# The third block of tokens, not the first, gets eight products; gated weights are converted one place sooner

## The chip, the cores and the metric

The kernel runs on one core of one Trainium2 chip. The metric is device time in microseconds (us), the median of several runs. The profile comes from one profiled execution, which had a time of its own.

## The reference

```python
# retention: q, k, v are (2, 8, 768, 64); a state of 64 x 64 a head, faded each step
state = gamma * state + einsum('bhd,bhe->bhde', k[:, :, t], v[:, :, t])
y[:, :, t] = scale * einsum('bhd,bhde->bhe', q[:, :, t], state)
x = y.transpose(0, 2, 1, 3).reshape(1536, 512)
# first network: w_in 512 x 2048, w_out 2048 x 512
h = x @ w_in
x = (maximum(h, 0) + log1p(exp(-abs(h)))) @ w_out
# second network: w_gate and w_val 512 x 1536, w_out 1536 x 512
rms = sqrt(mean(x * x, axis=-1) + 1e-6)
xn = x / rms * rms_g
g = xn @ w_gate
out = (g / (1 + exp(-g)) * (xn @ w_val)) @ w_out
```

The weights are stored in 64 bits, q, k, v and rms_g in 32.

## The kernel before, in words

The 1536 tokens are three blocks (b = 0, 1, 2) of 512. Every operand of a large product is split in a high and a low part in a rounded 32-bit format, and a product is three terms, high by high, high by low and low by high (TERMS). A weight tile comes as 64-bit words through one of three staging tiles; ScalarE (ACT), VectorE (DVE) and GpSimd (POOL) turn it into high and low parts in one of 11 or 12 slots (`convert`: `shift`, `bits`, `small`, `size`, `total`, `finish`, `high`, `rounded`).

The work is written out by hand as a row of pieces. A piece is one group of products on TensorE (PE), given to `piece()`, which lets due work go out (`run` by a running clock, `flush`), starts a conversion if asked (`conv`), and then writes the readers of the piece's products. Each engine takes its instructions in the order in which this writes them. A piece of 12 products advances that clock by 2.72, one of 6 by 1.36; it is only a due time for `later`.

Stage 1 is the retention. Stage 2 is the first network, in four groups (gr) of four of the 16 slices f of w_in and w_out: for each group and block four `l1` (w_in and softplus) and, one block behind, four `l2` (w_out, m = 0 to 3). The sums of block 0 stay in four PSUM banks through all groups (`keep`, list `kept`); those of blocks 1 and 2 are added up in SBUF (L556). After the last group `norm` takes the squares, their sum (`sums`, L593), the root of the mean (`mean`: a PE product, then 12 short DVE instructions), and spreads it over the partitions (`along`).

Stage 3 is the second network, in six rounds p of two slices. Blocks 1 and 2 share their products: for w_gate and for w_val seven products of half depth (`Seven`, p1 to p7) stand for the eight that two blocks need. They take sums of the weights (`combine`: tiles s, then ws_s) and sums and differences of the blocks (B11, B21, T1 to T4, B22), which `plain` and `mixing` make once, from `scaled` blocks. Block 0 is alone and takes its eight products (`l3`, tiles h_w_gate and h_w_val, four pieces a round); its rows are scaled after the product. `l4` multiplies by the second w_out, `to_g` splits its operand.

For an odd slice of w_gate or w_val `convert` asks for three free slots: its own and two for the sums. If a piece needs a weight that isn't ready, `need` writes all outstanding work of its conversion on the spot, ahead of the piece. `finish` is due 4.0 after the start, `high` 1.0 later, `combine` 0.9 after `finish`, and `parts` 2.7 after `combine`: there ACT takes the high parts of the sums, and DVE the low parts of both weights (L217, `rounded` on DVE). A round asks for conversions in pieces 0 and 2 of its `l3`, pieces 3 and 8 of w_gate's seven products and 2 and 8 of w_val's.

Of the kernel before, what the change touches and what calls it, by code (L numbers as in the profile page):

```python
# [20 lines left out]
G1 = 4  # L21
# [4 lines left out]
def retention_softplus_swiglu(ctx: ExitStack, tc: tile.TileContext, q, k, v, w_in, w_out,  # L26
# [133 lines left out]
    clock, due, raw = [0.0], [], {}  # L160
# [13 lines left out]
    def convert(parts=False):  # L174
# [6 lines left out]
        if len(free) < (3 if gated and f % 2 else 1):  # L181
            return False
# [26 lines left out]
        if gated and f % 2:  # L209
            sums, sa = [], [row(f"s{n}", "s") for n in range(2)]  # L210
            for n in range(2):
                slot["S", nm, f // 2, n] = free.pop(0)
                sums.append(rows(slot["S", nm, f // 2, n], f"ws_s{n}"))
                ws["S", nm, f // 2, n] = sums[n]
# [12 lines left out]
        def combine():  # L227
# [10 lines left out]
            def parts():  # L238
                for n in range(2):
                    high(sums[n], sa[n])  # L240
# [3 lines left out]
                ready.add(key)  # L244

# [5 lines left out]
            later(2.7, parts)  # L251
# [218 lines left out]
    bg = []  # L470
    normed = set()
# [48 lines left out]

    def l2_by(b, f):
        for m in range(KC):
# [3 lines left out]
            for n, (i, j) in enumerate(TERMS):  # L526
                nc.tensor.matmul(acc[b, m], lhsT=w[:, i, m * P:(m + 1) * P], rhs=g_t[b, f][:, j, :],  # L527
                                 start=(n == 0 and f == 0), stop=False)
        g_t.pop((b, f))
        return lambda: None  # L530

    def l2(b, gr, m):
        fs = range(gr * G1, (gr + 1) * G1)
        keep = b == 0
        if keep:
            p = acc[b, m]
        else:
            p = bank("l2")
# [10 lines left out]
        def after():  # L549
            if not keep:  # L550
                if gr == 0:
                    tags[b, m] = spin("s2_", 10)
                    acc[b, m] = row(tags[b, m], "x2")
                    nc.scalar.activation(out=acc[b, m], in_=p, func=AF.Copy)
# [14 lines left out]
    def norm(b, m):  # L569
        if m == 0:  # L570
            root[b], roots[b] = get("root") if b == 2 else (row(("r", "ms")[b], "root"), "ms")
            sqs[b] = [rows(f"at{2 * (b % 2) + n}", "sq", F32) for n in range(2)]
            if b == 0:
                channels(("n", b), b)
        sq, r = sqs[b], root[b]

        def high():
            if b == 0:
# [4 lines left out]
        def low():  # L583
# [3 lines left out]
            if m == KC - 1:  # L587
                normed.add(b)
# [23 lines left out]
        def along():  # L612
# [4 lines left out]
            rooted.add(b)  # L617

# [13 lines left out]
    TB, roots = {}, {}  # L632
    homes = {"B11": ("x4", "x5"), "B21": ("x6", "x7"), "T1": ("x8", "x9"), "B22": ("x10", "x11"),
# [19 lines left out]
    def mixing():  # L653
# [5 lines left out]
        def first():  # L659
            scaled(2, k1)  # L660
            for n in range(2):
                diff(acc[1, n], acc[2, n], acc[1, n])

        def second():
            for n in range(2):
                part_hi("T1", n, acc[1, n])
            scaled(2, k2)

        def third():
            for n in range(2):  # L670
                part_lo("T1", n, acc[1, n])
# [488 lines left out]
```

## Time and profile before

| | us |
|---|---|
| median of 3 runs (653.99 to 654.61) | 654.55 |
| profiled execution | 654.71 |
| its span | 653.0 |
| TensorE busy in the span | 613.4 (94%) |
| VectorE | 450.6 (69%) |
| ScalarE | 359.7 (55%) |
| GpSimd | 284.5 (44%) |

Stage 2 ends and stage 3 begins at about 325 us; the rounds of stage 3 follow each other from about 379 us to the end. The profile's busy time of TensorE counts a product from its start to its modelled end. Durations in the timeline overlap: a row of four instructions of 0.69 us that starts at 325.57, with the next row at 328.22, is 0.66 us from start to start. The granted clock is 1.00 at 2.4 GHz and 0.50 at 1.2 GHz.

### The profile page before, as it was taken

Reading aid. Unit: us, or ns where it says so; the run is one execution under the profiler, and the core shown is the slowest. Engines: PE = TensorE matmul, PEld = TensorE weight load, DVE = VectorE, ACT = ScalarE, POOL = GpSimd, SP = SyncE. Lnnn points to the kernel's source line nnn. Section 1 sums busy time; section 2 is a strip of 40 time slices with the busy share of each in tenths; the row PEclk is TensorE's granted clock in tenths of the full one; section 3 lists DMA queues with packets and bytes.
Section 4 is the critical chain, followed back from the end, with each engine's and each line's share of the span. In section 5 each row is a group of like instructions: output and inputs, shape, how many; then the busy total and the mean of one; then the engine's idle time right before and its main releaser. Section 6 shows DMA issues by size and latency. Waiting matters only on the chain.

```text
span 653.0 us, 8618 instructions
## 1 busy us (share of the span) xinstructions
PE 613.4 (94%) x3232; PEld 503.9 (77%) x3232; DVE 450.6 (69%) x645; ACT 359.7 (55%) x613; POOL 284.5 (44%) x236
## 2 busy tenths in 40 slices
PE   8999999999999999999957787998998998998997
PEld 7888888888888888888846465886886886886886
DVE  5787776777636763575568965489689579679635
ACT  3466677887747774775354644644543453544421
POOL 3444355454403440220053976267367358248210
PEclk9999999999999999999977987999998998999999
DMA  9997133232302230200011022222212121221014
GB/s 207 216 238 184 34 97 114 80 98 96 97 0 65 96 98 1 64 2 0 1 61 36 21 78 65 64 65 64 66 64 63 46 69 50 66 64 65 1 44 150
DMA packets 65562, 48.84 MB, mean 75 GB/s; under 512 B 39792, under 2 KB 60528, under 8 KB 65520
## 3 DMA queue, kind: packets, MB, share of 16 engines
q1 hardware_dynamic: 64320, 47.90, 26.1%
q8 instruction: 25, 0.41, 0.3%
q10 hardware_dynamic: 1200, 0.39, 0.2%
q14 instruction: 17, 0.14, 0.1%
HBM read 45.14 MB, written 3.15 MB: 74 GB/s over the span
## 4 chain that ended last, share of the span: by engine, by line
PE 79%; DVE 13%; POOL 5%; issue 1%; ACT 1%; DMA 1%; SPq 0%; DVEq 0%; POOLq 0%
PE h L478 20%; PE l L542 18%; PE l L858 12%; PE Q L760 9%; PE h_w_val L478 3%; PE R L760 3%; PE y L439 3%; PE W L760 2%; DVE a L254 2%; PE sc L387 2%; DVE g L738 2%; POOL c L204 2%; PE l L527 2%; PE pt L368 1%; DVE w L196 1%
## 5 line engine op out<-in xcount | busy, mean ns | idle before, releaser
L204 POOL TENSOR_TENSOR c<-w,c 128x512 uint32<-128x512 uint32 x68 | 87.8, 1292 | 182.2 <-DVE w L200 121.5
L478 PE MATMUL h<-x,ws_w_in 128*128 128x512 f32 x576 | 138.7, 390 | 0.0
L542 PE MATMUL l<-g,ws_w_out 128*128 128x512 f32 x528 | 126.5, 390 | 0.0
L478 PEld LDWEIGHTS h<-x,ws_w_in 128*128 128x128 f32 x576 | 107.7, 188 | 23.0 <-issue 0.7
L542 PEld LDWEIGHTS l<-g,ws_w_out 128*128 128x128 f32 x528 | 98.9, 188 | 20.5
L858 PE MATMUL l<-ws_w_out,g 128*128 128x512 f32 x432 | 113.1, 403 | 0.0
L858 PEld LDWEIGHTS l<-ws_w_out,g 128*128 128x128 f32 x432 | 84.7, 196 | 18.3
L516 DVE SCALAR_TENSOR_TENSOR t<-h,t 128x512 f32<-128x512 f32 x48 | 33.1, 690 | 72.1 <-ACT t L509 72.1
L217 POOL TENSOR_TENSOR ws_w_out<-a,ws_w_out 128x512 fp32r<-128x512 f32 x28 | 37.3, 1332 | 69.5 <-ACT ws_w_out L220 69.5
L254 DVE SCALAR_TENSOR_TENSOR a<-a,c 128x512 f32<-128x512 f32 x68 | 52.0, 765 | 18.0 <-POOL c L204 18.0
L478 PE MATMUL h_w_val<-x,ws_w_val 128*128 128x512 f32 x144 | 41.4, 436 | 22.6 <-DVE ws_w_val L217 21.7
L478 PEld LDWEIGHTS h_w_val<-x,ws_w_val 128*128 128x128 f32 x144 | 30.0, 213 | 32.2 <-DVE ws_w_val L217 24.2
L124 ACT ACTIVATE g<-t 128x512 fp32r<-128x512 f32 x48 | 30.3, 632 | 38.5 <-DVE t L516 38.5
L504 ACT ACTIVATE t<-h 128x512 f32<-128x512 f32 x48 | 28.7, 598 | 36.1 <-PE h L478 35.8
L125 DVE TENSOR_TENSOR g<-t,g 128x512 fp32r<-128x512 f32 x48 | 33.7, 704 | 12.3 <-ACT g L124 9.4
L760 PE MATMUL Q<-T,ws_s 128*128 128x512 f32 x144 | 37.3, 393 | 4.1 <-ACT p L766 1.6
L888 DVE TENSOR_TENSOR o<-l,o 128x512 f32<-128x512 f32 x39 | 26.7, 686 | 20.1 <-PE l L858 19.9
L781 POOL TENSOR_TENSOR t<-t,e 128x512 f32<-128x512 f32 x18 | 26.3, 1461 | 32.6 <-DVE e L777 32.6
L766 ACT ACTIVATE p<-Q 128x512 f32<-128x512 f32 x36 | 21.4, 596 | 32.9 <-PE Q L760 32.9
L478 PE MATMUL h_w_gate<-x,ws_w_gate 128*128 128x512 f32 x144 | 35.6, 397 | 2.6 <-DVE ws_w_gate L217 2.6
L737 ACT ACTIVATE g<-t 128x512 fp32r<-128x512 f32 x36 | 21.9, 626 | 28.3 <-DVE t L838 12.6
L217 POOL TENSOR_TENSOR ws_w_in<-a,ws_w_in 128x512 fp32r<-128x512 f32 x16 | 22.9, 1431 | 31.2 <-ACT ws_w_in L220 31.2
(132 smaller groups left out, 1071.5 us busy)
## 6 DMA issues: line engine op xcount, KB each, us to landing
st_w_out<-in_moe_w_out_dram SPq DMA_DIRECT2D x28, 512.0 KB, 3.3
st_w_in<-in_moe_w_in_dram SPq DMA_DIRECT2D x16, 512.0 KB, 3.8
st_w_gate<-in_moe_w_gate_dram SPq DMA_DIRECT2D x12, 512.0 KB, 3.7
st_w_val<-in_moe_w_val_dram SPq DMA_DIRECT2D x12, 512.0 KB, 3.5
v<-in_v_dram SPq DMA_DIRECT2D x12, 256.0 KB, 4.7
q<-in_q_dram SPq DMA_DIRECT2D x23, 128.0 KB, 4.6
k<-in_k_dram SPq DMA_DIRECT2D x23, 128.0 KB, 4.0
out_dram<-o SPq DMA_DIRECT2D x11, 256.0 KB, 2.0
```

What stands on the lines that cost most here:

```text
L124: nc.scalar.activation(out=hi, in_=src, func=AF.Copy)
L125: eng.tensor_tensor(out=lo, in0=src, in1=hi.bitcast(F32), op=ALU.subtract)
L204: nc.gpsimd.tensor_tensor(out=c, in0=w, in1=c, op=ALU.add)
L217: eng.tensor_tensor(out=out[:, 1], in0=src, in1=out[:, 0].bitcast(F32), op=ALU.subtract)
L254: nc.vector.scalar_tensor_tensor(out=a, in0=a, scalar=TINY, in1=c.bitcast(F32), op0=ALU.is_ge, op1=ALU.mult)
L478: nc.tensor.matmul(h, lhsT=w[:, i, kk * P:(kk + 1) * P], rhs=src[j][kk // 2][:, kk % 2, :], start=(n == 0), stop=(n == 3 * KC - 1))
L504: nc.scalar.activation(out=got[0], in_=h, func=AF.Abs)
L516: nc.vector.scalar_tensor_tensor(out=t, in0=h, scalar=0.0, in1=t, op0=ALU.max, op1=ALU.add)
L542: nc.tensor.matmul(p, lhsT=w[:, i, m * P:(m + 1) * P], rhs=g_t[b, f][:, j, :], start=(n == 0 and f == (0 if keep else fs[0])), stop=(n == ...
L760: nc.tensor.matmul(ps, lhsT=halves(w[:, i], p)[:, kk * P:(kk + 1) * P], rhs=t[j][:, kk, :], start=start and n == 0, stop=n == 5, skip_grou ...
L858: nc.tensor.matmul(ps4, lhsT=g_t[b, f][:, j, m * P:(m + 1) * P], rhs=w[:, i, :], start=n == 0 and (i, j) == TERMS[0], stop=n == 1 and (i, ...
L888: nc.vector.tensor_tensor(out=o, in0=ps4, in1=o, op=ALU.add)
```

## The change

Blocks 0 and 1 now share seven products, and block 2 is the lone one (LONE). Block 2's sums of stage 2 stay in PSUM; block 0's first group is copied to SBUF (`kept_row`, two copies on ACT and two on DVE). `mixing` has a list of its own (`mix`), starts four pieces after block 1's last `l2`, has eight steps for seven, and all its differences are on DVE: four differences and four low parts leave POOL. The first round of stage 3 begins with block 2's last `l2`, p1 and p2 of both weights, then the four `l3`. If the lone block's root isn't there, ACT copies the product first and the scaling waits (`waiting`).

A conversion asks for one free slot beyond those that are reserved; the sums' two slots are reserved at the start and taken in `parts`. The low parts of both weights (`whole`) are due 1.3 after `combine`, the sums' high parts 4.0. Two conversions move into the last step of stage 2. From round 1 on conversions stand in piece 2 of the `l3`, in the first `l4`, in pieces 3 and 8 of w_gate's products and 2 and 7 of w_val's.

```diff
-        if len(free) < (3 if gated and f % 2 else 1):
+        if len(free) - reserved[0] < 1:
...
-            def parts():
-                for n in range(2):
-                    high(sums[n], sa[n])
+            def whole():
                 for out, src in ((other, a0), (t, a1)):
                     rounded(out, src, nc.vector)
                 ready.add((nm, f - 1))
                 ready.add(key)
+
+            def parts():
+                reserved[0] -= 2
+                for n in range(2):
+                    slot["S", nm, f // 2, n] = free.pop(0)
+                    sums.append(rows(slot["S", nm, f // 2, n], f"ws_s{n}"))
+                    ws["S", nm, f // 2, n] = sums[n]
+                    high(sums[n], sa[n])
...
-            later(2.7, parts)
+            later(1.3, whole)
+            later(4.0, parts)
...
-        keep = b == 0
+        keep = b == NB - 1
...
-            bg.extend(([None, sums, None, mean, None, None, along],
-                       [None, sums, None, mean, None, along, plain],
+            bg.extend(([None, sums, None, mean, None, along, plain],
+                       [None, sums, mean, along],
                        [None, sums, None, mean, None, along])[b])
-            if b == 2:
-                bg.extend(mixing())
+            if b == 1:
+                mix.extend([None, None, None, None] + mixing())
...
+                if LONE in rooted:
+                    times(h)
+                else:
+                    nc.scalar.activation(out=t, in_=h, func=AF.Copy)
+                    waiting.setdefault(LONE, []).append(lambda: times(t))
...
-                    piece((l1s if kind == "1" else l2s).pop(0)(), n % 2 == 0 and (gr, b) != (NG1 - 1, NB - 1))
+                    piece((l1s if kind == "1" else l2s).pop(0)(), n % 2 == 0 and ((gr, b) != (NG1 - 1, NB - 1) or n in (2, 4)))
...
-            for n, one in enumerate(h[:2] + l2s + h[2:]):
-                piece(one(), n in (0, 6, 7))
+            for m in range(KC):
+                piece(l2(2, NG1 - 1, m), False)
+            for n, one in enumerate([g.p1, g.p2, v.p1, v.p2]):
+                piece(one(), n == 1, half)
+            for n, one in enumerate(h):
+                piece(one(), n in (1, 3))
...
-            piece(h[n](), n in (0, 2))
-            piece(L[n](), False, half)
+            piece(h[n](), n == 2)
+            piece(L[n](), n == 0, half)
...
-            piece(one(), n in (2, 8), half)
+            piece(one(), n in (2, 7), half)
```

TensorE from stage 2 to stage 3, before: the last four `l2` (here block 2's) have w_gate's lone products ahead of them and w_val's behind them.

```order
L542 MATMUL l_3063<-g,ws_w_out 128x512 x12
L599 MATMUL ms<-ones,sq 128x1 x4
L542 MATMUL l_3099<-g,ws_w_out 128x512 x12
L542 MATMUL l_3115<-g,ws_w_out 128x512 x12
L615 MATMUL root<-ident,root_t 128x128 x4
L542 MATMUL l_3136<-g,ws_w_out 128x512 x12
L478 MATMUL h_w_val<-x_2705,ws_w_val 128x512 x2
```

TensorE at the same place now: p1 of the shared products (Q from B) follows block 2's `l2`.

```order
L563 MATMUL l_3026<-g,ws_w_out 128x512 x12
L563 MATMUL l_3044<-g,ws_w_out 128x512 x12
L563 MATMUL l_1445<-g,ws_w_out 128x512 x12
L563 MATMUL l_1493<-g,ws_w_out 128x512 x12
L617 MATMUL ms<-ones,sq 128x1 x4
L563 MATMUL l_1541<-g,ws_w_out 128x512 x12
L633 MATMUL root<-ident,root_t 128x128 x4
L563 MATMUL l_1589<-g,ws_w_out 128x512 x12
L787 MATMUL Q<-B_3014,ws_w_gate 128x512 x2
```

The lone products have moved behind eight pieces more, and the statistics of block 1 (ms, root) stand between block 2's `l2`.

VectorE there, before: the low parts of B11 and B21 (L647), then a whole conversion of w_val's second slice.

```order
L647 TENSOR_TENSOR B_3156<-x_1312,B_3155 128x512
L647 TENSOR_TENSOR B_3156<-x_1362,B_3155 128x512
L647 TENSOR_TENSOR B_3162<-x_1388,B_3161 128x512
L647 TENSOR_TENSOR B_3162<-x_1406,B_3161 128x512
L196 TENSOR_SCALAR w<-st_w_val_2700 128x512
L200 SCALAR_TENSOR_TENSOR w<-st_w_val_2700,w 128x512
L254 SCALAR_TENSOR_TENSOR a<-a,c 128x512
L217 TENSOR_TENSOR ws_w_val<-a,ws_w_val 128x512 x2
```

VectorE now, from the low parts of B21 (B_3021) on; both slices of w_val have begun their conversion above.

```order
L667 TENSOR_TENSOR B_3021<-x_1268,B_3020 128x512
L667 TENSOR_TENSOR B_3021<-x_1270,B_3020 128x512
L258 SCALAR_TENSOR_TENSOR a<-a,c 128x512
L125 TENSOR_TENSOR g<-t,g 128x512
L575 TENSOR_TENSOR x_1396<-l_3026,x_1396 128x512
L575 TENSOR_TENSOR x_1414<-l_3044,x_1414 128x512
L214 TENSOR_TENSOR ws_w_val<-a,ws_w_val 128x512 x2
L611 TENSOR_TENSOR sq<-sq 128x1024
L612 TENSOR_TENSOR sq<-sq 128x512
```

The bit operations (L196, L200) of w_val stand no longer between B and the low parts of w_val.

VectorE in round 2, before: from the low parts of w_gate to those of w_val (o is the output, e and t the gated products).

```order
L890 SCALAR_TENSOR_TENSOR o<-l_3926,root_t,o 128x512
L777 TENSOR_TENSOR e<-R,p_3871 128x512
L254 SCALAR_TENSOR_TENSOR a<-a,c 128x512
L196 TENSOR_SCALAR w<-st_w_val_3859 128x512
L200 SCALAR_TENSOR_TENSOR w<-st_w_val_3859,w 128x512
L723 TENSOR_TENSOR t<-h_w_gate,root 128x512
L888 TENSOR_TENSOR o<-l_3979,o 128x512
L254 SCALAR_TENSOR_TENSOR a<-a,c 128x512
L738 TENSOR_TENSOR g<-t,g 128x512 x2
L723 TENSOR_TENSOR t<-h_w_gate,root 128x512
L888 TENSOR_TENSOR o<-l_4013,o 128x512
L217 TENSOR_TENSOR ws_w_val<-a,ws_w_val 128x512 x2
```

VectorE in round 2 now, the last instructions ahead of the low parts of w_val and the two behind them.

```order
L765 TENSOR_TENSOR g<-t,g 128x512
L917 SCALAR_TENSOR_TENSOR o<-l_3946,root_t,o 128x512
L258 SCALAR_TENSOR_TENSOR a<-a,c 128x512
L804 TENSOR_TENSOR e<-R,p_3893 128x512
L745 TENSOR_TENSOR t<-h_w_gate,root 128x512
L214 TENSOR_TENSOR ws_w_val<-a,ws_w_val 128x512 x2
L196 TENSOR_SCALAR w<-st_w_out_3877 128x512
L200 SCALAR_TENSOR_TENSOR w<-st_w_out_3877,w 128x512
```

The pair of low parts has moved ahead of the reader of the second h_w_gate (L723 before, L745 now), and the second conversion (L196, L200) far above it.

## Rows read from the trace of the kernel before

**Rows 1.** Page, part 2: TensorE busy tenths and granted clock, 40 slices.
```profile
PE   8999999999999999999957787998998998998997
...
PEclk9999999999999999999977987999998998999999
```

**Rows 2.** Chain of work, 300 to 480 us: start, us, what.
```profile
301.28 0.44 PE root L615 x4
301.71 5.47 PE l L542 x24
...
315.35 0.79 PE ms L599 x8
...
324.94 0.02 issue
...
407.28 1.36 PE Q L760 x6
```

**Rows 3.** Timeline of TensorE: start, us, what, [idle before it <-releaser].
```profile
334.56 5.85 PE L478 MATMUL h_w_val<-x,ws_w_val 128*128 128x512 f32 x16 [7.82 <-DVE ws_w_val L217]
...
346.47 1.87 PE L599 MATMUL ms<-ones,sq 128*128 128x1 f32 x8 [3.34 <-DVE sq L594]
...
398.06 2.08 PE L478 MATMUL h_w_val<-x,ws_w_val 128*128 128x512 f32 x4 [3.40 <-DVE ws_w_val L217]
...
439.76 1.52 PE L858 MATMUL l<-ws_w_out,g 128*128 128x512 f32 x6
```

**Rows 4.** Tile h_w_val from 430 us: what ended its engine's idle time.
```profile
  DVE ws_w_val L217: 10.4, 4
```

**Rows 5.** Windows: TensorE, its loads, DVE, ACT, POOL busy, TensorE clock, DMA.
```profile
364.00:368.00 4.00, 2.35 (x9) 1.61 (x9) 3.85 (x3) 1.75 (x4) 4.00 (x4) 1.00 0.00 0
...
440.77:457.10 16.33, 13.72 (x61) 11.05 (x60) 15.72 (x19) 6.60 (x12) 12.13 (x11) 1.00 0.20 64
489.75:506.07 16.32, 13.71 (x53) 10.83 (x53) 15.13 (x18) 6.39 (x11) 12.12 (x11) 0.90 0.22 63
538.73:555.05 16.32, 13.71 (x54) 10.81 (x52) 15.97 (x19) 6.22 (x11) 13.59 (x11) 0.90 0.15 49
587.70:604.02 16.32, 13.71 (x56) 10.89 (x55) 15.28 (x18) 7.50 (x13) 14.28 (x11) 0.92 0.19 65
```

**Rows 6.** Timeline of VectorE (DVE), same columns.
```profile
303.27 0.69 DVE L516 SCALAR_TENSOR_TENSOR t<-h,t 128x512 f32<-128x512 f32 x1 [2.76 <-ACT t L509]
...
310.55 1.22 DVE L593 TENSOR_TENSOR sq<-sq 128x1024 f32<-128x1024 f32 x1
...
316.17 0.16 DVE L601 TENSOR_SCALAR small<-ms 128x4 f32<-128x4 f32 x1
...
318.34 0.16 DVE L610 SCALAR_TENSOR_TENSOR root_t<-small,root_t 128x4 f32<-128x4 f32 x1
...
325.57 2.73 DVE L638 SCALAR_TENSOR_TENSOR x<-x,rg,root 128x512 f32<-128x512 f32 x4
328.22 2.49 DVE L647 TENSOR_TENSOR B<-x,B 128x512 fp32r<-128x512 f32 x4
...
361.54 3.29 DVE L647 TENSOR_TENSOR T<-x,T 128x512 fp32r<-128x512 f32 x2
...
372.93 0.68 DVE L773 TENSOR_TENSOR t<-R,p 128x512 f32<-128x512 f32 x1
...
443.92 0.68 DVE L723 TENSOR_TENSOR t<-h_w_gate,root 128x512 f32<-128x512 f32 x1
...
449.03 1.84 DVE L217 TENSOR_TENSOR ws_w_val<-a,ws_w_val 128x512 fp32r<-128x512 f32 x2
```

**Rows 7.** Timeline of GpSimd (POOL), same columns.
```profile
358.45 9.22 POOL L657 TENSOR_TENSOR x<-x,x 128x512 f32<-128x512 f32 x4 [3.15 <-DVE x L638]
```

**Rows 8.** Page, part 5: the 68 integer sums of conversions on GpSimd.
```profile
L204 POOL TENSOR_TENSOR c<-w,c 128x512 uint32<-128x512 uint32 x68 | 87.8, 1292 | 182.2 <-DVE w L200 121.5
```

**Rows 9.** Page, part 6: loads of w_gate: KB each, us from issue to landing.
```profile
st_w_gate<-in_moe_w_gate_dram SPq DMA_DIRECT2D x12, 512.0 KB, 3.7
```

More of the change, by code (lines that the diff above doesn't have):

```diff
@@ L519, in l1, with kept_row @@
         return after
+    def kept_row(b, m, src):
+        tags[b, m] = spin("s2_", 10)
+        acc[b, m] = row(tags[b, m], "x2")
+        if m % 2 and b == 0:
+            nc.vector.tensor_copy(acc[b, m], src)
+        else:
+            nc.scalar.activation(out=acc[b, m], in_=src, func=AF.Copy)
     def l2_by(b, f):
@@ L527, in l2_by, with after @@
                 nc.tensor.matmul(acc[b, m], lhsT=w[:, i, m * P:(m + 1) * P], rhs=g_t[b, f][:, j, :],
-                                 start=(n == 0 and f == 0), stop=False)
+                                 start=(n == 0 and f == 0), stop=(n == 2 and f == G1 - 1))
         g_t.pop((b, f))
-        return lambda: None
+        def after():
+            if f == G1 - 1:
+                for m in range(KC):
+                    kept_row(b, m, acc[b, m])
+                lend()
+        return after
     def l2(b, gr, m):
         fs = range(gr * G1, (gr + 1) * G1)
-        keep = b == 0
+        keep = b == NB - 1
         if keep:
+            if gr == 0:
+                acc[b, m] = bank("l2", kept)
             p = acc[b, m]
@@ L570, in norm @@
         if m == 0:
-            root[b], roots[b] = get("root") if b == 2 else (row(("r", "ms")[b], "root"), "ms")
+            root[b] = row(("r", "ms", "r")[b], "root")
             sqs[b] = [rows(f"at{2 * (b % 2) + n}", "sq", F32) for n in range(2)]
-            if b == 0:
+            if b == LONE:
                 channels(("n", b), b)
@@ L617, in along @@
             rooted.add(b)
+            for do in waiting.pop(b, ()):
+                do()
         def plain():
@@ L693, in sixth, with eighth @@
             for n in range(2):
-                part_lo("T3", n, acc[2, n], nc.gpsimd)
+                part_lo("T3", n, acc[1, n])
         def seventh():
             for n in range(2):
-                part_lo("T4", n, acc[1, 2 + n])
+                part_lo("T4", n, acc[0, 2 + n])
+        def eighth():
             for n in range(2):
-                part_lo("B22", n, acc[2, 2 + n], nc.gpsimd)
-            two.extend(tags[b, m] for b in (1, 2) for m in range(KC))
-            two.extend((roots[1], roots[2]))
-        return [first, second, third, fourth, fifth, sixth, seventh]
+                part_lo("B22", n, acc[1, 2 + n])
+            two.extend(tags[b, m] for b in (0, 1) for m in range(KC))
+            two.append("ms")
+        return [first, second, third, fourth, fifth, sixth, seventh, eighth]
     two, wide_o = [], []
@@ L1080, in retention_softplus_swiglu @@
         if p == 0:
-            l2s = [lambda m=m: l2(2, NG1 - 1, m) for m in range(KC)]
-            for n, one in enumerate(h[:2] + l2s + h[2:]):
-                piece(one(), n in (0, 6, 7))
-            later(0.4, gs_of(p, 0))
-            for n, one in enumerate([g.p1, g.p2, v.p1, v.p2] + l4s(0, 0) + [g.p5, v.p5, g.p6, v.p6, g.p7, v.p7, g.p4, v.p4]):
-                if n == 9:
-                    later(0, lambda: to_g(1, 0))
-                piece(one(), n in (12,), half)
-            later(0.4, lambda: to_g(1, 1))
@@ L1090, in retention_softplus_swiglu @@
-            piece(g.p3(), True, half)
-            piece(v.p3(), False, half)
+            for m in range(KC):
+                piece(l2(2, NG1 - 1, m), False)
[3 more added lines that the diff above has]
+                piece(one(), n in (1, 3))
+            later(0.4, gs_of(p, LONE))
+            L = l4s(0, LONE)
+            for n, one in enumerate([g.p5, v.p5, g.p6, v.p6, L[0], g.p7, v.p7, L[1], g.p4, v.p4, L[2], g.p3, v.p3, L[3]]):
+                if n == 6:
+                    later(0, lambda: to_g(0, 0))
+                if n == 11:
+                    later(0, lambda: to_g(0, 1))
+                piece(one(), n in (2, 6, 10), half)
```

105 lines of the change are left out of this document (51 added, 54 removed).

## The prediction

> **What bounds the kernel now.** I read the strip of 40 slices first, to see where TensorE isn't full. Its busy digits are 8 or 9 up to slice 20, fall to 5, 7, 7, 8, 7 in the five that follow (326 to 408 us), and from there to the end every third slice is an 8 [rows 1]. In the five slices the granted clock falls too (7, 7, 9, 8, 7). So there are two losses: a large one where stage 3 begins, and a small one in each round. Everything ahead of 325 us is bound by TensorE and has nothing to give.
>
> The first loss comes from the chain of waits. Up to 324.94 it is TensorE, and from 407.28, where the first shared product of round 1 begins, TensorE again without a gap [rows 2]. Between lie 82.3 us. The products in them are 24 of w_val and 48 of round 1 (`l3`), 24 of p1 and p2, 60 of p3 to p7 and 48 of `l4`: 204. The chain has 24 in 5.47 us, 0.228 each, so 46.5 us; with one group of sums (0.79) and one spread root (0.44), 47.7 [rows 2]. The loss is 82.3 - 47.7 = 34.6 us, idle time and clock together. TensorE's timeline names the largest stops: 7.82 us for w_val's low parts, 3.34 for the sum of squares, 3.40 for w_val's low parts in round 1 [rows 3]. All wait for VectorE, which does the scaling, B11, B21 and a whole conversion one after the other.
>
> The second loss: the tile h_w_val has from 430 us on four stops of 10.4 us in all, again until w_val's low parts [rows 4], one in each of rounds 2 to 5. The windows around them show 13.71 us busy of 16.32, and in three of the four a granted clock of 0.90, 0.90 and 0.92, part of the slice at 1.2 GHz instead of 2.4: 1.63 + 1.63 + 1.31 = 4.6 us more [rows 5]. Together 15.0 us. Stops of less than 2 us each, as at 364 to 368, leave the clock at 1.00 [rows 5].
>
> The sum goes against the profiled execution, 654.7 us, with 1.7 outside its span; the median of the three runs is 0.16 below it, which the rounding covers.
>
> **Part 1, stage 2: 0.** Block 0's four copies are new and block 2's four are gone; block 0 has the twelve additions in SBUF that block 2 had. Pairs of pieces that convert and add at once came four in a row in each group, and come eight in a row now. Such a pair has six VectorE instructions, at 0.60 to 0.66 us (below) under 4, beside 24 products or 5.5 us, so nothing piles up. I take 0, from -1 to +1.
>
> **Part 2, the start of stage 3.** TensorE's work is the same 47.7 us in another order. What decides is whether VectorE keeps up: it now has block 1's statistics, block 2's, the lone block's low parts and `mixing` in one run, and the eight instructions that left POOL. I count from the end of the last `l1` product of stage 2, 301.28 before [rows 2]. VectorE's reader of it starts 2.0 us later, at 303.27 [rows 6]. In the new order 61 large instructions and two chains of 12 short ones follow it, up to the low part of the second operand of `l4` (L765).
>
> From start to start the rows give: two wide sums of squares, 1.22 each; 15 with two tensors and a scalar (scaling, the lone block's low parts, a conversion's last) at (328.22 - 325.57)/4 = 0.66; the other 44 at 0.60, as four low parts in 2.49, the last 0.69 long; a short chain 2.3 (316.17 to the end of 318.34) [rows 6]. Sum 2.4 + 9.9 + 26.4 + 4.6 = 43.3 us.
>
> To this come waits inside the list (the sums on TensorE stand behind products, ACT's high parts come first): 0 to 3, I take 1.5. And collisions with POOL: two low parts took 3.29 us while POOL had four differences of 9.22, against 1.2 alone; an addition that reads PSUM took 0.68 beside POOL [rows 6, 7]. POOL has 12 instructions beside this list, at most 1.29 each [rows 8], 15.5 us; in these VectorE at 1.6 us does 10 instructions for 25 and loses 10 us at most. I take half, 5, since short chains, PSUM readers and waits fall there too. VectorE is done at 2.0 + 43.3 + 1.5 + 5 = 51.8.
>
> TensorE wants that operand after six `l2`, four groups of p1 and p2, four `l3` and four half groups: 168 products, 38.3 us, with two sums and two spread roots 40.8, and some 0.7 into `l4`: 41.5. So it comes 10.3 us late; ends are 3.8 (no waits, no collisions) and 16.8 (3 and 10). TensorE stops for this in several places: at block 2's first `l2` for its last operand's low part, at the sums of block 1, at the spread root behind the first h_w_gate (the other three `l3` queue behind it), before `l4`. These don't add to the 10.3; they are parts of it, since all wait for the one list.
>
> A fallen clock ahead of `l4` costs nothing, because VectorE sets the pace; one behind it costs 1.6, as in a round [rows 5]; ends 0 and 3.3, I take 1.6. Copies of p6 and p7 on ACT stand behind conversions: 0 to 2, I take 0.8. Behind `l4`, VectorE has 11 instructions up to the low parts of round 1's w_gate, 6.6 us, and TensorE ten half groups, 13.7. The loads on SP's queue move with the conversions: a staging tile's next conversion stands six half groups later, 8.2 us, and a load lands in 3.7 [rows 9], so 0; without that cover ACT would stand some 2 us.
>
> The gain of part 2 is 34.6 - 10.3 - 1.6 - 0.8 = 21.9 us.
>
> The Trainium skill, GPSIMD Engine Reference, section 8, Key points, says that GpSimd shares its SBUF interfaces with VectorE and contends with instructions that have two SBUF inputs. That speaks against a change that puts eight of these on VectorE; the 3.29 against 1.2 agrees, and by that rule in full, with every microsecond of POOL's 15.5 colliding, the lateness would be 15.3 and the forecast 623.
>
> **Part 3, rounds 2 to 5.** Before, the pair of w_val's low parts stands behind the readers of both h_w_gate and ends at 450.9. VectorE came to the first reader at 443.92, though its product was there by 439.76 [rows 3, 6]: 4.2 us behind. Now w_gate's pair and the first conversion of w_val stand six half groups (8.2 us) sooner, the second conversion 6.8. Ahead of the first reader VectorE is thus relieved of that pair, 1.84 like this one, and of four instructions of 0.6: 4.2, the same as the lag, and more where POOL runs beside them. The pair then needs 0.6 and 1.84 [rows 6] from the end of the first h_w_gate; until h_w_val TensorE has 24 products, 5.5 us. Slack 3.0. So the four stops go, and the clock's falls with them: 15.0, from 13 to 15; I take 14.4, as a short stop may stay. Next late is nothing that the rows show; the low parts of the weights' sums stand 20 us ahead of their products. The tail is the same, 0.
>
> **Sum.** 654.7 - 21.9 - 14.4 = 618.4, so 618.
>
> **The rivals.**
> 1. VectorE's list hardly holds TensorE up: 3.8 late, no fallen clock, no copies. 654.7 - (34.6 - 3.8) - 15.0 = 608.9. For it: if POOL's work falls beside chains and PSUM readers, nothing collides. Against: three conversions lie in the list, each with POOL's sum in the middle.
> 2. The stop of each round only moves: VectorE is busy 15.97 of 16.32 in such a window [rows 5] and its work a round is the same, so that low parts which are early make something else late, as `l4`'s operands. The 14.4 isn't gained: 632.8. Against: the slack of 3.0.
> 3. Slower: VectorE and POOL collide all through the start of stage 3. Of the 61 instructions 49 read SBUF alone, and each that takes 1.6 for 0.6 costs 1.0. All 49 add 44 to the 5 in the sum: 662. It decides from 42 of 49. For it: each conversion moved here brings POOL along. Against: 15.5 us of POOL's work can't lie beside 49 of them.
>
> **How the numbers follow.** Forecast 0.74, its own range 611 to 629 (lateness 16.8, clock 3.3, copies 2 and 13 of the rounds' 15 at the upper end); rival 1 0.11, rival 2 0.11, rival 3 0.04. The range from 608 to 632 holds the forecast, most of rival 1 and part of rival 2. A measurement of this kernel can tell about 0.2% from no change. Only rival 3 gives a slower kernel, and near its deciding point no change: faster 0.95, same 0.01, slower 0.04.
>
> **What would show it.** Right: no stop of TensorE over 4 us at the start of stage 3, the wait of h_w_val for its low parts gone, the first shared product of round 1 some 22 us sooner than 407, the rounds full at clock 1.00, and VectorE without idle time from about 304 to 353. Wrong: stops at h_w_val or `l4` in the rounds (rival 2), low parts of T at 1.6 us throughout (rival 3), or a stop ahead of 300 us (part 1).

## The result and the profile after

| | before | after |
|---|---|---|
| median, us | 654.47 (4 runs) | 633.33 (4 runs, 632.48 to 634.37) |
| ratio | | 0.9679 (0.9662 to 0.9696) |
| profiled execution, span | 654.71, 653.0 | 632.48, 630.8 |

The kernel is 21.1 us faster; 36.3 were predicted (21.9 and 14.4). The time lies above the range by 1.3 us.

The strip of 40 slices after, TensorE's busy tenths and its granted clock:

```profile
PE   9999999999999999999897899899999999999997
...
PEclk9999999999999999999988999999999999999999
```

The hole in slices 21 to 25 is shallower than in [rows 1], and the clock's fall is down to two 8s. After it only slice 26 (394 to 410 us, in round 1) is an 8; the last digit is the tail.

TensorE's timeline after, its stops from stage 3's start to round 2 (start, duration, what, idle time before it and what ended it):

```profile
312.33 5.07 PE L563 MATMUL l<-g,ws_w_out 128*128 128x512 f32 x14 [1.92 <-DVE g L125]
318.88 1.02 PE L617 MATMUL ms<-ones,sq 128*128 128x1 f32 x8 [1.47 <-DVE sq L612]
339.90 0.65 PE L633 MATMUL root<-ident,root_t 128*128 128x128 f32 x4 [3.23 <-DVE root_t L628]
357.67 0.96 PE L885 MATMUL l<-ws_w_out,g 128*128 128x512 f32 x3 [1.35 <-DVE g L765]
359.37 0.73 PE L885 MATMUL l<-ws_w_out,g 128*128 128x512 f32 x2 [0.73 <-DVE g L765]
366.56 1.66 PE L787 MATMUL Q<-T,ws_w_val 128*128 128x512 f32 x6 [0.95 <-ACT p L793]
389.82 1.52 PE L787 MATMUL Q<-B,ws_w_gate 128*128 128x512 f32 x6
397.18 1.66 PE L787 MATMUL Q<-T,ws_s 128*128 128x512 f32 x6 [1.76 <-ACT p L793]
401.02 1.20 PE L787 MATMUL Q<-T,ws_s 128*128 128x512 f32 x4 [0.80 <-ACT p L793]
420.55 1.65 PE L787 MATMUL Q<-T,ws_w_val 128*128 128x512 f32 x6 [1.54 <-ACT p L793]
468.97 1.65 PE L787 MATMUL Q<-T,ws_w_val 128*128 128x512 f32 x6 [1.53 <-ACT p L793]
```

The stops of 7.82, 3.34 and 3.40 [rows 3] are gone, none is over 3.23, and the wait of h_w_val for its low parts [rows 4] has no successor. The first shared product of round 1 starts at 389.82 instead of 407.28: 17.5 sooner, where 21.9 were predicted. From it to the end of the span are 630.8 - 389.82 = 241.0 us, before 653.0 - 407.28 = 245.7: 4.7 less, where 14.4 were predicted. So most of what is missing between the two profiled executions, 9.7 of 14.1, lies in the rounds. The last four rows say what is new there: TensorE waits for ScalarE's copy L793, in four stops of about 1.5 at w_val's p4, one in each of rounds 1 to 4 (two are shown), and in round 1 at w_gate's p6 and p7 too.

Window after (TensorE, its loads, DVE, ACT, POOL busy, clock, DMA): round 2 from one h_w_gate to the next:

```profile
424.78:473.18 48.40, 46.82 (x205) 38.15 (x204) 41.76 (x51) 22.85 (x41) 28.82 (x23) 1.00 0.21 66
```

The rounds are at full clock, as forecast, but not full: a round is 34 half groups at 1.36 us, 46.2, and takes 48.4.

Why the copy is late stands in the rows of ScalarE, VectorE and GpSimd, in this order:

```profile
415.22 0.58 ACT L793 ACTIVATE p<-Q 128x512 f32<-128x512 f32 x1
419.38 0.63 ACT L217 ACTIVATE ws_w_val<-a 128x512 fp32r<-128x512 f32 x1 [3.58 <-DVE a L258]
419.92 0.58 ACT L793 ACTIVATE p<-Q 128x512 f32<-128x512 f32 x1
...
417.57 1.78 DVE L258 SCALAR_TENSOR_TENSOR a<-a,c 128x512 f32<-128x512 f32 x1
...
417.05 3.43 POOL L214 TENSOR_TENSOR ws_s<-s,ws_s 128x512 fp32r<-128x512 f32 x2
```

The second copy, of p7, has its product by 417.7, but ScalarE stands idle for 3.58 us ahead of it: the high part of a weight comes first, and that waits for VectorE's scaling (L258). The high part is wanted by the next round's h_w_val, 13 us later, the copy at once. p4 adds into the bank that is being copied and must wait.

VectorE's own lateness has a part in this. It was busy without a gap from 410.96 to 420.0, and four entries of its row there (L214, L196, L765, L258) took 1.93, 1.51, 1.41 and 1.78 beside GpSimd's work, where like ones in this trace took 1.28, 0.42, 0.69 and 0.68: 3.6 us more, longer than the stop. No run takes these away, so how much of the stop would go with them isn't shown.

### The profile page after: what moved, and what is told of

The parts are those of the page before. It is cut to its first block, busy times and chain, and to the rows that moved or that the text cites. A ratio compares the mean times of both kernels' runs of the same rounds, so it can differ in the third digit from the quotient of the medians.

```text
span 630.8 us, 8631 instructions
## 1 busy us (share of the span) xinstructions
PE 605.5 (96%) x3232; PEld 498.3 (79%) x3232; DVE 459.3 (73%) x655; ACT 355.5 (56%) x612; POOL 275.0 (44%) x228
## 4 chain that ended last, share of the span: by engine, by line
PE 57%; DVE 26%; ACT 8%; issue 4%; POOL 2%; SPq 2%; DMA 1%; DVEq 0%; POOLq 0%; ACTq 0%
PE h L483 18%; PE l L563 15%; PE l L885 6%; PE Q L787 5%; DVE g L765 4%; DVE w L200 3%; DVE a L258 3%; PE y L443 2%; DVE w L196 2%; PE R L787 2%; PE l L540 2%; PE sc L391 1%; DVE ws_w_gate L214 1%; SPq L84 1%; DVE ws_w_val L214 1%
## 5 line engine op out<-in xcount | busy, mean ns | idle before, releaser
L563 PE MATMUL l<-g,ws_w_out 128*128 128x512 f32 x528 | 129.8, 397 | 1.9 <-DVE g L125 1.9
L563 PEld LDWEIGHTS l<-g,ws_w_out 128*128 128x128 f32 x528 | 101.2, 192 | 23.7 <-DVE g L125 2.2
L885 PE MATMUL l<-ws_w_out,g 128*128 128x512 f32 x432 | 109.3, 390 | 2.1 <-DVE g L765 2.1
L885 PEld LDWEIGHTS l<-ws_w_out,g 128*128 128x128 f32 x432 | 81.0, 188 | 20.0 <-DVE g L765 2.8
L214 POOL TENSOR_TENSOR ws_w_out<-a,ws_w_out 128x512 fp32r<-128x512 f32 x28 | 38.8, 1387 | 50.5 <-ACT ws_w_out L217 50.5
L258 DVE SCALAR_TENSOR_TENSOR a<-a,c 128x512 f32<-128x512 f32 x68 | 52.8, 776 | 9.3 <-POOL c L204 9.3
L765 DVE TENSOR_TENSOR g<-t,g 128x512 fp32r<-128x512 f32 x36 | 41.5, 1176 | 11.1 <-ACT g L764 8.2
L125 DVE TENSOR_TENSOR g<-t,g 128x512 fp32r<-128x512 f32 x48 | 33.8, 707 | 13.0 <-ACT g L124 10.3
L214 POOL TENSOR_TENSOR ws_s<-s,ws_s 128x512 fp32r<-128x512 f32 x24 | 41.0, 1727 | 4.6 <-ACT ws_s L217 4.6
L808 POOL TENSOR_TENSOR t<-t,e 128x512 f32<-128x512 f32 x18 | 27.8, 1544 | 33.9 <-DVE e L804 33.9
L483 PE MATMUL h_w_gate<-x,ws_w_gate 128*128 128x512 f32 x144 | 36.3, 403 | 0.0
L233 POOL TENSOR_TENSOR s<-a 128x256 f32<-128x256 f32 x24 | 21.3, 887 | 32.2 <-DVE a L258 32.2
L787 PEld LDWEIGHTS Q<-T,ws_s 128*128 128x128 f32 x144 | 26.7, 188 | 10.2 <-ACT p L793 4.8
```

What stands on the lines that cost most here:

```text
L125: eng.tensor_tensor(out=lo, in0=src, in1=hi.bitcast(F32), op=ALU.subtract)
L214: eng.tensor_tensor(out=out[:, 1], in0=src, in1=out[:, 0].bitcast(F32), op=ALU.subtract)
L258: nc.vector.scalar_tensor_tensor(out=a, in0=a, scalar=TINY, in1=c.bitcast(F32), op0=ALU.is_ge, op1=ALU.mult)
L483: nc.tensor.matmul(h, lhsT=w[:, i, kk * P:(kk + 1) * P], rhs=src[j][kk // 2][:, kk % 2, :], start=(n == 0), stop=(n == 3 * KC - 1))
L563: nc.tensor.matmul(p, lhsT=w[:, i, m * P:(m + 1) * P], rhs=g_t[b, f][:, j, :], start=(n == 0 and f == (0 if keep else fs[0])), stop=(n == ...
L765: nc.vector.tensor_tensor(out=g[:, 1], in0=t, in1=g[:, 0].bitcast(F32), op=ALU.subtract)
```

## The experiments

All were compared with the kernel before; a ratio is against it. Blocks of a diff are against the changed kernel unless said otherwise.

**1. The high part one half group later**

```diff
-                later(1.0, high)
+                later(2.2, high)
```

> The changed kernel with the high part of a gated weight due 2.2 us after its scaling instead of 1.0, so one half group later; ScalarE then has the copy of p7 ahead of the high part in each round of w_val. Theory Q (the copy stands behind a high part that waits for VectorE's scaling): the four stops of 1.54, 1.53, 1.53 and 1.52 us at the fourth product of w_val in rounds 1 to 4 go, with the some 0.3 us that TensorE needs after each; 633.3 becomes 626 to 627. Rival V (ScalarE is only the messenger; VectorE's or GpSimd's load makes something else late by as much): a stop of like size stands in another place of the round, time 632 to 634.

629.96, ratio 0.9626 (0.9594 to 0.9658): 3.4 gained, half of what Q expected. TensorE's timeline:

```profile
312.17 3.47 PE L563 MATMUL l<-g,ws_w_out 128*128 128x512 f32 x14 [1.93 <-DVE g L125]
318.72 1.84 PE L617 MATMUL ms<-ones,sq 128*128 128x1 f32 x8 [3.08 <-DVE sq L612]
320.42 5.28 PE L563 MATMUL l<-g,ws_w_out 128*128 128x512 f32 x12
...
449.95 1.65 PE L787 MATMUL Q<-T,ws_s 128*128 128x512 f32 x6 [0.86 <-ACT p L793]
```

The stop at p4 of w_val is gone, so Q has the place right. But one of 0.86 has come at p7 of w_gate, so V is right that something else is next. The first three rows show more by chance. In the changed kernel's profiled run these 14 products took 5.07, at a granted clock of 0.66, and the stop behind them was 1.47; here they took 3.47 at 1.00 and the stop is 3.08. Both end at 318.7 to 318.9, so up to there the fallen clock cost nothing, as the prediction had it. But here the fall came behind the longer stop: the 12 products there took 5.28, at a granted clock of 0.67 from 318.72 to 328.74 (4.59 in the changed kernel's profile), and the first h_w_gate came at 335.12 instead of 333.78.

**2. The rounds' part alone, on the kernel before** (against before)

```diff
-            piece(h[n](), n in (0, 2))
-            piece(L[n](), False, half)
+            piece(h[n](), n == 2)
+            piece(L[n](), n == 0, half)
...
-            piece(one(), n in (2, 8), half)
+            piece(one(), n in (2, 7), half)
```

with `whole`, `parts` and the reserved slots as changed.

> The kernel before, with only the third part of the change: whole low parts before the sums' high parts, slots taken when written, conversions in rounds 1 to 5 at the new places. Block order and start of stage 3 as before. Prediction as put (14.4 gained, no new stop): 654.5 becomes 640. Theory Q: the stops at h_w_val go (rounds 2 to 5 take 9.9 us less, as in the changed kernel's trace) and the copy's stop of 1.5 comes in rounds 1 to 4. If round 1's other loss in the changed kernel (5.2 us against the same stretch before, of which 2.6 in two stops at p6 and p7 of w_gate) is a backlog of the start of stage 3, it isn't here: 646 to 647. If it belongs to the conversions' new places: 649 to 650.

653.64, ratio 0.9979 (0.9965 to 0.9994). All three expectations fail: the stops at h_w_val are there as before.

```profile
447.91 1.20 PE L482 MATMUL h_w_val<-x,ws_w_val 128*128 128x512 f32 x4 [2.69 <-DVE ws_w_val L214]
```

The table of places doesn't say which weight is converted at a place; that goes by how many conversions came ahead. The changed kernel has two conversions more by the end of round 0 (eight against six, counted from w_val's first), and so each place of a round works on a later weight. Without them the second w_val is still converted in the next round's `l3`. That is theory G, which the next two tell.

**3. Block order alone**: conversion routine and rounds' places of before, and one conversion less asked for in round 0 (the old rule of three free slots puts off another, so two fewer are done by its end).

```diff
-                piece(one(), n in (2, 6, 10), half)
+                piece(one(), n in (4, 9), half)
```

> The changed kernel's block order and start of stage 3, with the conversion routine of before and one conversion less in round 0, so that rounds 1 to 5 convert the same weight at the same place as before. Theory G (the place at which w_val is converted, which one conversion more in round 0 moves, is what frees h_w_val; the rest is the start): the stops of 2.6 us at h_w_val come back in rounds 2 to 5 with part of the clock's falls, the copies' stops go, and the start's 17.5 us remain: 654.5 - 17.5 = 637, 635 to 639. Rival H (the block order itself frees h_w_val, since the spread roots and differences lie otherwise): no stop at h_w_val, under 630.

646.38, ratio 0.9876 (0.9856 to 0.9896).

```profile
332.72 1.22 PE L783 MATMUL Q<-B,ws_w_val 128*128 128x512 f32 x2 [7.64 <-DVE ws_w_val L217]
...
398.60 1.52 PE L783 MATMUL Q<-B,ws_w_gate 128*128 128x512 f32 x6
...
490.50 2.01 PE L479 MATMUL h_w_val<-x,ws_w_val 128*128 128x512 f32 x4 [2.71 <-DVE ws_w_val L217]
```

For the rounds G holds: h_w_val waits again and no copy does. For the start, and with it for the time (635 to 639), it doesn't: the first w_val is late by 7.64, and round 1's first shared product starts at 398.60, so of the start's 17.5 us 8.7 are left. The sooner conversions, with their routine, are worth as much there as the block order.

**4. Two conversions sooner, in the order of before**: experiment 2's kernel and

```diff
-                piece(one(), n in (12,), half)
+                piece(one(), n in (2, 8, 12), half)
```

> The kernel before in its own block order, with the third part of the change and three conversions in round 0's half groups instead of one, so that in rounds 1 to 5 the weights are converted at the changed kernel's places. Theory G: no stop at h_w_val, the copy's stops of 1.5 in rounds 1 to 4 as in the changed kernel; rounds 2 to 5 take 9.9 us less and round 1 some 2 more, the start as before within 3: 646 to 650 (644 to 653 with the start). The prediction's own size for this part: 640. Rival H: the stops at h_w_val stay, 652 to 655.

645.74, ratio 0.9859 (0.9842 to 0.9876). G holds.

```profile
402.09 1.52 PE L764 MATMUL Q<-B,ws_w_gate 128*128 128x512 f32 x6
...
481.71 1.65 PE L764 MATMUL Q<-T,ws_w_val 128*128 128x512 f32 x6 [1.54 <-ACT p L770]
485.94 2.88 PE L482 MATMUL h_w_gate<-x,ws_w_gate 128*128 128x512 f32 x12
...
534.35 2.88 PE L482 MATMUL h_w_gate<-x,ws_w_gate 128*128 128x512 f32 x12
```

No stop at h_w_val in rounds 2 to 5, the same stop at p4 of w_val, the same round of 534.35 - 485.94 = 48.4. From 402.09 to the end of its span (643.5) are 241.4 us, 4.3 less than before, as the changed kernel has 4.7 less; the rest of the 9.0 came at the start. Round 1 has the stops at p6 and p7 of w_gate too (2.27 and 0.82). So the new waits belong to the conversions' places and not to the block order or a backlog of the start.

**5. The readers of a product first**

```diff
     def piece(after, conv=1, us=2.72):
         clock[0] += us
+        first = us == 1.36 and not bg and not mix
+        if first:
+            after()
         run()
...
-        after()
+        if not first:
+            after()
```

> The changed kernel, but from round 0's half groups on what reads a product's PSUM (ScalarE's copies of p1, p6, p7 among it) is issued ahead of that place's conversion steps, not behind them. Theory Q (in ScalarE's row the copies stand behind steps that wait for VectorE): both stops of a round go, at p7 of w_gate and at p4 of w_val, and rounds 1 to 4 take 46.3 to 46.8 us from one h_w_gate to the next instead of 48.4; round 1's first stops shrink. 633.3 becomes 622 to 626. Rival V (VectorE and GpSimd are behind in each round, so that a copy that is early only moves the stop): as with the high part moved alone, 629 to 631.

629.97, ratio 0.9634 (0.9611 to 0.9657): V's time. In its profile, of its fastest execution (628.26), what is gained lies ahead of round 2; a later round takes 48.2. TensorE, ScalarE and VectorE:

```profile
446.52 1.66 PE L787 MATMUL Q<-T,ws_s 128*128 128x512 f32 x6 [1.67 <-ACT p L793]
...
444.24 0.63 ACT L801 ACTIVATE t<-t 128x512 f32<-128x512 f32 x1 [1.64 <-DVE t L800]
444.77 0.65 ACT L190 ACTIVATE c<-st_w_gate 128x512 uint32<-128x512 uint32 x1
445.33 0.66 ACT L193 ACTIVATE a<-st_w_gate 128x512 f32<-128x512 f32 x1
445.88 0.58 ACT L793 ACTIVATE p<-Q 128x512 f32<-128x512 f32 x1
...
443.52 0.68 DVE L800 TENSOR_TENSOR t<-W,p 128x512 f32<-128x512 f32 x1
```

The stop has moved whole to p7 of w_gate. Its copy of p6 could go at 443.5; ahead of it stands the Silu (L801), which waits for VectorE's sum, and two conversion steps behind that. So it is the same mechanism one place on, and not yet VectorE's pace.

**6. The Silu later**: experiment 5's kernel and

```diff
-                later(0.5, lambda: nc.scalar.activation(out=t, in_=t, func=AF.Silu))
+                later(4.0, lambda: nc.scalar.activation(out=t, in_=t, func=AF.Silu))
```

> The kernel with the copies first (629.97 us), and the Silu of a shared product of w_gate due 4.0 us after its sum instead of 0.5, so two to three half groups later. Theory Q, second form (what holds the copy of p6 in that kernel is ScalarE's Silu ahead of it, which waits for VectorE's sum; the value isn't needed for ten half groups): the stops of 1.67, 1.70 and 1.67 us at p7 of w_gate go, a round takes 46.3 to 46.8 us, 629.97 becomes 621 to 624. Rival V (VectorE's list is the pace of a round): the stop moves once more, a round stays at 48, 628.5 to 630.5.

622.11, ratio 0.951 (0.9488 to 0.9531): Q in its second form holds, V falls. In round 0 of this kernel and of experiment 11's the Silu comes after its product is taken, so the function is another there; in experiment 7 it is at its old place.

**7. The same, round 0's Silu at its old place**

```diff
+                later(4.0 if self.p else 0.5, lambda: nc.scalar.activation(out=t, in_=t, func=AF.Silu))
```

> The kernel with the copies first and the Silu late, but with round 0's Silu at its old place (in the one before, round 0's Silu came behind its product); it computes the whole reference. Theory Q: the rounds are full as there, 46.2 us from one h_w_gate to the next, and the time is the same 622 (621 to 623.5). Rival: the Silu in round 0 was what held TensorE at the start, and its old place costs 1 us or more again, 623.5 to 625.

620.77, ratio 0.9473 (0.9453 to 0.9492): the lowest time of all. Experiment 6 lies 1.3 higher, but in its profile VectorE waited 1.85 for block 1's spread root and here 0.27, in code that is the same up to there (more on this wait below), so that 1.3 can't be put down to round 0's Silu. The first shared product of round 1, and a round from one h_w_gate to the next:

```profile
389.00 1.52 PE L787 MATMUL Q<-B,ws_w_gate 128*128 128x512 f32 x6
...
465.71 2.88 PE L483 MATMUL h_w_gate<-x,ws_w_gate 128*128 128x512 f32 x12
...
511.95 2.88 PE L483 MATMUL h_w_gate<-x,ws_w_gate 128*128 128x512 f32 x12
```

A round takes 46.24, no stop is left in rounds 2 to 5, and from the first shared product of round 1 to the end of the span (619.0) are 230.0 us: 15.7 less than before, where the prediction had 14.4 of a possible 15.0.

**8. The start: the root later**

```diff
-                       [None, sums, None, mean, None, along])[b])
+                       [None, sums, None, mean, None, None, along])[b])
```

> The changed kernel with the lone block's spread root one group later in TensorE's row, behind the second h_w_gate; the stop of 3.23 us at that root and the half clock behind it should shrink or go. Theory L (VectorE's list sets when the operand of l4 is there, the stops ahead of it are parts of one lateness): the time that is saved there is lost again at l4, total 632.5 to 634. Rival S (each stop costs its own time): 3.2 + 2.0 of clock are gained, 628 to 629.

633.5, ratio 0.9674 (0.965 to 0.9699): L holds. The stop at the root fell from 3.23 to 0.51, and `l4` stops for 4.96 in its place:

```profile
339.74 0.65 PE L633 MATMUL root<-ident,root_t 128*128 128x128 f32 x4 [0.51 <-DVE root_t L628]
...
356.25 0.79 PE L885 MATMUL l<-ws_w_out,g 128*128 128x512 f32 x1 [4.96 <-ACT g L764]
```

**9. The start: no differences** (the body of `diff` is empty)

> The changed kernel without the eight differences of the mixing (VectorE instructions of 0.64 us, 5.1 us in all, at the start of stage 3); the operands of the shared products are then not differences. Nothing else is left out. Theory L (VectorE's list sets the pace there): l4's operand is 5 us sooner and the whole kernel 4.5 to 6 us shorter, 627 to 629. Rival T (TensorE's order and its clock set it, VectorE has room): under 2 us, 631.5 to 633.5.

629.38, ratio 0.9624 (0.9593 to 0.9654): 3.9 gained, between L's 4.5 to 6 and T's under 2, and nearer L; with executions from 628.46 to 634.13 the time alone excludes neither. The profiled executions tell more: the list, from its first reader to its end, took 51.6 instead of 54.0, and the time is 2.4 lower too. Of the 5.1 taken out, 2.3 came back as longer waits of VectorE: 0.8 for the sums on TensorE, 0.2 for the root, 1.25 for ScalarE's squares.

**10. The start: w_gate's conversion later**: experiment 5's kernel with `piece(one(), n == 1)` for the `l3` and places (1, 5, 8, 11).

> As the one with the copies first, and in round 0 the first conversion of w_gate 2 places later (behind the scaling and low parts that l4 waits for on VectorE), the three behind it 1 to 3 places later too. Theory L (VectorE's list up to l4's second operand sets the pace): the two instructions of 1.1 us and the collision beside them leave the list, l4 starts 1 to 2.5 us sooner, and the time is 1 to 2.5 below the kernel with the copies first. Rival: the weights' low parts are late for round 1's h_w_gate or h_w_val, a stop of 2 us or more there, and the time is no lower.

632.45, ratio 0.9655 (0.9637 to 0.9674): no lower than experiment 5, whose executions (628.26 to 632.89) overlap with these (631.57 to 633.11). The stops at `l4` shrink from 2.1 to 0.9, and one of 1.42 comes at h_w_val for its low parts. So the rival's stop is there, if smaller than its 2 us. But VectorE's wait for block 1's spread root, ahead of all that was changed, was 2.76 in this profile and 0.28 in experiment 5's, as much as the 2.5 between the medians: whether L's gain is hidden behind it isn't decided.

**11. The start: low parts behind**: experiment 6's kernel, three empty steps ahead of `seventh`.

> As the one with the Silu late, and at the start of stage 3 the low parts of T4 and B22 (four VectorE instructions that took 2.06 and 1.28 us) behind the two low parts that l4 waits for. Theory L (VectorE's list up to l4's second operand sets the pace): l4 starts 2.5 to 3.3 us sooner and the time is as much lower than with the Silu late alone. Rival: p4 or p3 then waits for T4 or B22, or the sums of block 2 set the pace, under 1 us.

622.42, ratio 0.9505 (0.9481 to 0.9528), the same as experiment 6. The lone block's `l4` no longer stops; the next one, for block 0, does, by 1.72 and 0.32. The time is the rival's, the place neither's.

**12. The start: GpSimd quiet**

> The changed kernel with ten GpSimd instructions taken out of the start of stage 3: the sums of the first w_val pair and their low parts (ScalarE writes copies instead), and the integer sums and low parts of the first two w_out2 (its low parts copies by ScalarE). These sums and parts are then not the ones that the products should have; VectorE's instructions are all there. Theory C (VectorE's instructions beside GpSimd's took 1.65 to 2.07 instead of 0.6 to 1.28, 5 to 6 us over the list): they fall to 0.69 and 1.28, the list ends 4.5 to 6 us sooner and the kernel takes 3.5 to 5 less, 628 to 630. Rival (they are long for another reason, or their time is hidden): within 1.5 of 633.3.

626.04, ratio 0.9561 (0.9542 to 0.958): 7.3 gained, more than C expected. VectorE and GpSimd in the changed kernel:

```profile
313.40 1.98 DVE L214 TENSOR_TENSOR ws_w_val<-a,ws_w_val 128x512 fp32r<-128x512 f32 x2
315.31 1.75 DVE L611 TENSOR_TENSOR sq<-sq 128x1024 f32<-128x1024 f32 x1
317.09 1.65 DVE L612 TENSOR_TENSOR sq<-sq 128x512 f32<-128x512 f32 x1
...
356.17 3.15 DVE L765 TENSOR_TENSOR g<-t,g 128x512 fp32r<-128x512 f32 x2
...
315.94 3.92 POOL L214 TENSOR_TENSOR ws_s<-s,ws_s 128x512 fp32r<-128x512 f32 x2
```

and VectorE's same instructions with GpSimd quiet:

```profile
314.01 1.28 DVE L215 TENSOR_TENSOR ws_w_val<-a,ws_w_val 128x512 fp32r<-128x512 f32 x2
315.21 1.22 DVE L622 TENSOR_TENSOR sq<-sq 128x1024 f32<-128x1024 f32 x1
316.47 0.69 DVE L623 TENSOR_TENSOR sq<-sq 128x512 f32<-128x512 f32 x1
...
350.62 1.92 DVE L776 TENSOR_TENSOR g<-t,g 128x512 fp32r<-128x512 f32 x2
```

The list ends at 352.5 instead of 359.3, 6.8 sooner; from its first reader it takes 46.6 instead of 54.0. Of these 7.4, the collisions make 6.0 (all VectorE rows of the two lists compared), and 1.6 is the wait for block 1's spread root, 0.27 here and 1.86 there. This is why more was gained than C expected.

**13. The start: the sums later**: experiment 7's kernel, the first w_val pair's `combine` due 9.0 after `finish`, `whole` 2.2 after `finish`.

> As the one just before, but GpSimd's sums of the first w_val pair and their two low parts (8.1 us of GpSimd) some three groups later, behind block 1's sums of squares and beside its short chain. Theory C (what counts is which of VectorE's instructions lie beside GpSimd's): low parts and sums of squares that took 1.98, 1.75 and 1.65 us take 1.28, 1.23 and 0.69, and short instructions and PSUM readers lose nothing: the list ends 1.5 to 2.2 us sooner and the time is 1 to 2 lower than that of the one just before. Rival M (the collisions only move to the scaling and the differences behind): within 0.7 of it, or p5's wait for the late sums makes it slower.

620.81, ratio 0.9473 (0.9454 to 0.9492): as experiment 7. VectorE and GpSimd:

```profile
312.22 1.29 DVE L214 TENSOR_TENSOR ws_w_val<-a,ws_w_val 128x512 fp32r<-128x512 f32 x2
...
332.90 3.16 DVE L674 TENSOR_TENSOR T<-x,T 128x512 fp32r<-128x512 f32 x2
...
333.78 3.40 POOL L214 TENSOR_TENSOR ws_s<-s,ws_s 128x512 fp32r<-128x512 f32 x2
```

w_val's low parts have their 1.29, but T1's now take 3.16. Rival M's time holds, and the collisions move with GpSimd's work.

## Why the prediction was wrong

**Part 3 failed in one sentence: "Next late is nothing that the rows show."** The sum was right: the four stops of h_w_val went, the clock stayed at 1.00, and with the copies out of the way the stretch gives 15.7 (experiment 7). But what took the place of the stops was ScalarE's row. I looked at VectorE and at SP's queue for each moved conversion, and priced ScalarE's copies of p6 and p7 only at the start (0.8, from 0 to 2; 0.95 came there). I didn't count that a moved conversion also puts its high part, a wait for VectorE, ahead of a copy that TensorE waits for. Measured: about 2.2 us in each of rounds 1 to 4 (48.4 against 46.2), and in round 1, whose shared products ran without a gap before, two stops of 2.56 more. Experiments 4, 5 and 6 show it: the same stop comes with the same conversions in the old block order, moves one place when the copy alone is freed, and goes when nothing that waits stands ahead of a copy. Rival 2 was the nearest in number, with "low parts which are early make something else late" and 632.8, but by luck: it named `l4`'s operands, which the rounds don't wait for, and put the rounds at 0 (4.7 came) and the start at 21.9 (17.5 came).

The reason given for the slack, four instructions and a pair of low parts fewer ahead of the first reader, holds only because two conversions more go ahead of round 0's end: experiment 2 has the new places without them, and no slack.

**Part 2 failed in a size, the lateness of VectorE's list (10.3), and in one sentence: "A fallen clock ahead of `l4` costs nothing, because VectorE sets the pace".** The last l1 product ends at 302.3 in the changed kernel, the list at 359.3: 57.0 us, not 51.8. With the 41.5 of TensorE's work that makes 15.5 late, within the ends of 3.8 and 16.8 but not near the middle. Three terms were small. Collisions cost 7.7 and not 5: the four VectorE rows of experiment 12, against 1.28, 1.22, 0.69 and 1.28 undisturbed, are 4.1 of it, four more between 334 and 352 the rest. Waits inside the list were 3.1 (1.21 for the sums, 1.86 for the root) and not 1.5, and the first reader came 3.0 and not 2.0 after the product, as VectorE's rows after show:

```profile
305.33 0.69 DVE L521 SCALAR_TENSOR_TENSOR t<-h,t 128x512 f32<-128x512 f32 x1 [2.51 <-ACT t L514]
...
319.94 0.16 DVE L619 TENSOR_SCALAR small<-ms 128x4 f32<-128x4 f32 x1 [1.21 <-PE ms L617]
...
325.46 1.42 DVE L658 SCALAR_TENSOR_TENSOR x<-x,rg,root 128x512 f32<-128x512 f32 x2 [1.86 <-ACT root L634]
```

The 1.86 is TensorE's clock. The root that VectorE waits for (block 1's) stands behind 12 products, which took 4.59 here, at a granted clock of 0.68 from 318.88 to 324.19. In experiment 7's profile, with the same instructions up to there, they took 3.01 at 1.00. TensorE after, then TensorE and VectorE in experiment 7:

```profile
319.76 4.59 PE L563 MATMUL l<-g,ws_w_out 128*128 128x512 f32 x12
...
319.07 3.01 PE L563 MATMUL l<-g,ws_w_out 128*128 128x512 f32 x12
...
323.18 1.42 DVE L658 SCALAR_TENSOR_TENSOR x<-x,rg,root 128x512 f32<-128x512 f32 x2 [0.27 <-ACT root L634]
```

With the wait at 0.27 the waits are the 1.5 of the forecast, and the list from its first reader takes 52.4 and not 54.0. So the engine that sets the pace waited for TensorE itself. Nor does a stop of less than 2 us always leave the clock at 1.00: here it was 0.66 behind one of 1.92 and 0.68 behind one of 1.47. Of the 5.2 more lateness, 2.7 are collisions, 1.6 the clock by way of the root, 1.0 the first reader. Experiment 12 shows the first two, in its rows. The clock's 1.6 behind `l4` didn't come. The sum, 15.5 and 0.95 instead of 12.7, makes 3.8 of the 4.4 missing there; the last l1 product ended 1.0 later than before (0.51 of it a stop at block 0's root), the upper end of part 1's 0, from -1 to +1.

The rule of the Trainium skill that was weighed (GPSIMD Engine Reference, section 8, Key points: GpSimd contends with VectorE's instructions that have two SBUF inputs) agrees with experiment 12, where such an instruction falls from 1.65 to 0.69. By it in full the collisions would have been 10 and the lateness 15.3. The 15.5 measured is near that by luck: the collisions were 7.7, and half of what came on top of 10.3 was the wait and the first reader.

**Right:** that the parts of the list's lateness don't add up (experiment 8: a stop of 3.2 taken away, nothing gained), that the clock's fall behind the lone block's root is free (there 12 products took 4.58 after and 3.02 in experiment 7, where `l4` then stopped 1.63 at its first product), that the low parts of h_w_val would be in time, and that no stop at the start is over 4 us.

**Open:** whether the start can be shortened by order alone. Four reorderings of it (experiments 8, 10, 11, 13) gave nothing that can be told, but VectorE's wait for block 1's root went from 0.27 to 2.76 between the profiles of these kernels, so that a gain of 1 or 2 us could be hidden. What decides between the two clock levels in an execution is open as well.

## What to carry to other kernels

When an instruction that waits is moved, read the row of every engine that it issues to, and ask what stands behind it that TensorE needs at once; a copy out of an accumulating PSUM bank belongs ahead of anything that can wait. When a table says at which places a step runs, count what comes ahead of the table: the places can stay and the content of each still shift. Where one engine's list sets the end of a stretch, less work in the list helped here (experiments 9 and 12) and no reordering was seen to; count its collisions in, and its waits for products of an engine whose clock may have fallen.

## What the runs showed of the hardware

One VectorE instruction with two SBUF inputs (L612) took 1.65 us beside GpSimd's low parts and 0.69 without, and moving the work that causes it out of one place brought it back at another (experiment 13): a pair of low parts took 3.16 beside GpSimd's two (3.40) and 1.28 alone. The Trainium skill (SBUF — State Buffer, Terms) says that of the two engines the later one blocks for the whole of the other's instruction. The 1.88 us more of that pair, beside two instructions of 1.7 each, are of that order; that each block lasts a whole instruction the rows don't show. The granted clock after a like stop differed between executions at the same place of the program: 14 products behind a stop of 1.92 took 5.07 in the changed kernel's profile (granted clock 0.66) and 3.47 behind one of 1.93 in experiment 1's (1.00). At the next such place 12 products took 4.59 and 3.01 behind stops of 1.47 and 1.48, in the changed kernel's profile and experiment 7's.
